# A gated linear attention layer and its GELU MLP on one core: a scheduled two-stage kernel rewritten as a hand-ordered two-phase pipeline with transposes by DMA

## The chip, the cores and the metric

The kernel runs on one core of a Trainium2 chip. The core has five engines with instruction streams of their own: PE (TensorE, matrix products; PEld is its loading of weights), ACT (ScalarE), DVE (VectorE), POOL (GpSimd) and SP (SyncE, which here only issues DMAs). Sixteen DMA engines carry out the transfers that SP and POOL issue. The metric is device time in microseconds (us), as the median of several executions; lower is better.

## The reference

Inputs are q, k, v and alpha of shape (batch 4, heads 8, sequence 768, head size 48) in float32, and two weights, w_in (384 x 2048) and w_out (2048 x 384). The heads of the result lie side by side and make rows of 384 for the MLP:

```python
for t in range(S):                       # S = 768, per batch and head
    state = alpha[t][:, None] * state + outer(k[t], v[t])      # 48 x 48
    y[t]  = q[t] @ state
x = y.transpose(0, 2, 1, 3).reshape(3072, 384)
h = x @ w_in                             # 3072 x 2048
g = 0.5 * h * (1 + tanh(c * (h + 0.044715 * h**3)))
out = g @ w_out                          # 3072 x 384
```

## The kernel before, in words

The sequence is cut into chunks of 128 steps. A unit is one chunk of one batch element with all 8 heads: 6 chunks by 4 batch elements are 24 units, taken in the order "all four batch elements of chunk 0, then of chunk 1, ...". With b the running product of alpha inside a chunk, a unit computes q' = q b and k' = k / b, the masked scores (k' q'^T, causal), y = scores v + q' state, and the new state = (state + k'^T v) b_end.

The kernel has two stages one after the other, and then a drain.

- **Decays, all units at once** (lines 99 to 122). For each pair of units alpha is loaded by POOL (L105), its logarithm is taken on ACT (L108, with a constant MU folded in against overflow), and PE sums it along the chunk with a triangular matrix `ut` (L114, tile `cumla`) and per head with a column of ones (L118). DVE keeps the sums in `cum_all` (L120), ACT keeps exp of the end sums in `bend_all` (L121). `w_in` and `w_out` are loaded by SP in float32 (L93, L130) and cast to bf16 by DVE (L127, L159).
- **Units in a three-step software pipeline** (lines 146 to 178). Stage a loads q, k, v by POOL (L190). Stage b makes exp of the sums on ACT (L200, L202), the products q' and k' on DVE (L205, L206), casts v on ACT (L208), and transposes q' and k' per head on PE (L213, L214), with a copy out of PSUM by ACT (L215) and DVE (L216). Stage c makes the scores on PE (L234), masks them on DVE (L237, tile `atm`), makes y and the state's increment on PE (L241, L243, L245), updates the state on DVE (L249, L250), copies y to `x_sb` on ACT (L255), transposes it on PE (L259) and copies it on DVE into `xT_all` (L260).
- **The MLP** runs in groups of four units (512 rows) as a list of pieces: 16 first-layer pieces (three matmuls L275 into `hT`, GELU on ACT L279 into `gT`) and 4 second-layer pieces (16 matmuls L286 into `acc`, a DVE copy L291, an SP store L293). After each unit up to 7 pieces are popped from the list; what is left is drained at the end.

Instructions are written in this order, and a scheduler sets the final order on each engine. Buffers come from pools; the PSUM buffers `tT_ps`, `ybank` and `acc` are single.

## Time and profile before

| what | value |
|---|---|
| time, median of 3 runs | 298.85 us (297.84 to 299.3) |
| span of the profiled execution, first to last instruction | 295.8 us |
| median time less that span | 3.05 us |
| busy: PE, ACT, DVE, POOL | 224.5, 200.8, 141.3, 87.4 us |
| DMA: bytes moved, mean rate over the span | 30.22 MB, 102 GB/s |

The page gives no time of its own for the profiled execution, only its span; the 3.05 us are what the timed runs hold beside such a span. Busy time is what an engine spent in instructions; matmuls overlap in the pipeline, so the mean duration of one (379 ns for L275) is longer than the distance from one to the next. "Idle before" is the engine's idle time just ahead of a group of instructions, with what ended it. The chain of waits follows the last instruction back to what released it. "L275" is line 275 of the kernel.

### The profile page before, as it was taken

What the parts mean: (1) busy time and instruction counts of PE and PEld (TensorE: products, weight loads), DVE (VectorE), ACT (ScalarE), POOL (GpSimd) and SP (SyncE); (2) the same over time, 40 slices, a digit from 0 to 9 for tenths busy, and PEclk for the clock granted to TensorE, in tenths of its full rate; (3) what the DMA queues carried; (4) which work ended last, traced back from release to release, by engine and by line L of the source; (5) the groups of instructions that cost most, each with busy time, mean ns of one, the idle gap of its engine ahead of it and who ended that gap; (6) DMA issues with size and microseconds to landing.
All of it is one profiled execution on the core that took longest, in us unless ns stands there. A gap on an engine that the chain in (4) does not pass through costs nothing.

```text
span 295.8 us, 5241 instructions
## 1 busy us (share of the span) xinstructions
PE 224.5 (76%) x2112; PEld 132.8 (45%) x2112; DVE 141.3 (48%) x274; ACT 200.8 (68%) x301; POOL 87.4 (30%) x114
## 2 busy tenths in 40 slices
PE   0043333332778989899998999999999999999983
PEld 0022212221656535556556555565456644554441
DVE  7183433222599855567548144656243633540011
ACT  0257787978677999996999999945761276304800
POOL 9643321005988758153333213220000000000000
PEclk9999999999999999999999999999999999999999
DMA  7999951002999979373232512241001100011011
GB/s 278 283 187 274 291 126 53 0 1 67 193 187 187 189 144 198 89 181 99 80 82 59 182 53 55 53 109 53 2 1 55 53 2 0 3 53 55 0 53 54
DMA packets 12168, 30.22 MB, mean 102 GB/s; under 512 B 2032, under 2 KB 7152, under 8 KB 11760
## 3 DMA queue, kind: packets, MB, share of 16 engines
q0 software_dynamic: 6144, 18.88, 30.4%
q1 hardware_dynamic: 6000, 11.01, 11.0%
q8 instruction: 16, 0.26, 0.4%
q14 instruction: 8, 0.07, 0.1%
HBM read 25.17 MB, written 4.72 MB: 101 GB/s over the span
## 4 chain that ended last, share of the span: by engine, by line
PE 47%; ACT 34%; DMA 7%; DVE 6%; issue 3%; POOL 1%; SPq 0%; DVEq 0%; POOLq 0%; ACTq 0%
PE acc L286 16%; PE hT L275 15%; ACT gT L279 6%; ACT L279 5%; ACT L108 4%; DMA w_in_f<-in_moe_w_in_dram 4%; ACT qT_ring L215 3%; PE kT_ps L214 3%; PE qT_ps L213 3%; ACT la L108 3%; PE at_ps L234 2%; ACT L200 2%; ACT L202 2%; ACT L121 2%; DVE w_in_sb L127 2%
## 5 line engine op out<-in xcount | busy, mean ns | idle before, releaser
L275 PE MATMUL hT<-xT_all,w_in_sb 128*128 128x512 bf16 x288 | 74.5, 379 | 4.0 <-ACT gT L279 3.8
L286 PE MATMUL acc<-w_out_sb,gT 128*128 128x384 bf16 x384 | 70.8, 326 | 3.0 <-DVE ot L291 2.8
L279 ACT ACTIVATE gT<-hT 128x512 bf16<-128x512 f32 x96 | 55.5, 598 | 16.3 <-PE hT L275 14.2
L286 PEld LDWEIGHTS <-gT 128*128 128x128 bf16 x384 | 36.4, 97 | 28.0 <-issue 4.0
L114 PE MATMUL cumla<-la,ut 128*128 128x384 bf16 x24 | 11.6, 485 | 48.3 <-ACT la L108 39.1
L291 DVE COPY ot<-acc 128x384 f32<-128x384 f32 x24 | 13.3, 555 | 53.6 <-PE acc L286 53.6
L237 DVE TENSOR_TENSOR atm<-at_ps,ut 128x512 bf16<-128x512 f32 x48 | 31.1, 683 | 15.9 <-PE at_ps L234 15.7
L275 PEld LDWEIGHTS <-w_in_sb 128*128 128x128 bf16 x288 | 24.8, 97 | 26.3 <-issue 5.5
L118 PEld LDWEIGHTS <-la 128*48 128x48 bf16 x192 | 9.5, 129 | 55.5 <-issue 55.5
L190 POOL DMA_DIRECT2D q<-in_q_dram x24 | 21.2, 884 | 44.1 <-PE cumla L118 24.1
L120 DVE CAST cum_all<-cumla 128x384 f16<-128x384 f32 x24 | 13.3, 556 | 32.5 <-PE cumla L118 32.5
L190 POOL DMA_DIRECT2D v<-in_v_dram x24 | 21.2, 885 | 25.3 <-ACT v8b L208 21.8
L105 POOL DMA_DIRECT2D a<-in_alpha_dram x24 | 21.5, 900 | 21.3 <-ACT la L108 18.9
L215 ACT COPY qT_ring<-qT_ps 64x1024 bf16<-64x1024 bf16 x24 | 24.1, 1005 | 4.9 <-PE qT_ps L213 4.6
L190 POOL DMA_DIRECT2D k<-in_k_dram x24 | 21.2, 885 | 18.3 <-DVE kp_ring L206 17.4
L208 ACT CAST v8b<-v 128x384 bf16<-128x384 f32 x24 | 12.3, 512 | 18.7 <-PE yps L243 17.9
L216 DVE COPY kT_ring<-kT_ps 64x1024 bf16<-64x1024 bf16 x24 | 16.3, 680 | 17.5 <-PE kT_ps L214 17.1
L108 ACT ACT_TABLE_LOAD x11 | 14.1, 1283 | 13.4 <-DMA a<-in_alpha_dram 13.2
L213 PE MATMUL qT_ps<-ident,qp_ring 128*64 128x128 bf16 x192 | 18.3, 230 | 5.9 <-DVE qp_ring L205 5.3
L205 DVE TENSOR_TENSOR qp_ring<-q,b 128x384 bf16<-128x384 f32 x24 | 13.2, 551 | 14.6 <-PE at_ps L234 5.7
L213 PEld LDWEIGHTS <-qp_ring 128*64 128x64 bf16 x192 | 12.7, 114 | 16.5 <-issue 14.9
L255 ACT CAST x_sb<-yps 128x384 bf16<-128x384 f32 x24 | 11.4, 476 | 12.7 <-PE yps L243 10.6
(49 smaller groups left out, 319.2 us busy)
## 6 DMA issues: line engine op xcount, KB each, us to landing
a<-in_alpha_dram POOLq DMA_DIRECT2D x24, 192.0 KB, 7.2
q<-in_q_dram POOLq DMA_DIRECT2D x24, 192.0 KB, 5.3
k<-in_k_dram POOLq DMA_DIRECT2D x24, 192.0 KB, 5.7
v<-in_v_dram POOLq DMA_DIRECT2D x24, 192.0 KB, 5.2
out_dram<-ot SPq DMA_DIRECT2D x24, 192.0 KB, 1.9
w_in_f<-in_moe_w_in_dram SPq DMA_DIRECT2D x3, 1024.0 KB, 7.4
w_out_f<-in_moe_w_out_dram SPq DMA_DIRECT2D x4, 768.0 KB, 12.4
```

Source lines behind the costliest of these rows:

```text
L105: nc.gpsimd.dma_start(a8[:, i], alpha[b].rearrange("h s d -> s h d")[tsl])
L108: nc.scalar.activation(la8, a8, AF.Ln, scale=float(math.exp(-MU)))
L120: nc.vector.tensor_copy(cum_all[:, tt, :], cumla)
L190: nc.gpsimd.dma_start(t_sb, t_dram[b].rearrange("h s d -> s h d")[tsl])
L213: nc.tensor.transpose(qT_ps[:, h, :], qp[:, h, :], ident)
L215: nc.scalar.copy(qT[0:64], qT_ps)
L216: nc.vector.tensor_copy(kT[0:64], kT_ps)
L237: nc.vector.tensor_tensor(atm, at_ps, ut[:, None, :].to_broadcast([C, 4, C]), op=ALU.mult)
L275: nc.tensor.matmul(hT, w_in_sb[:, j, nt * C:(nt + 1) * C], xsl, start=(j == 0), stop=(j == NKT - 1),)
L279: nc.scalar.activation(gT[:, nt, :], hT, AF.Gelu_apprx_tanh)
L286: nc.tensor.matmul(acc, gT[:, nt, mt * C:(mt + 1) * C], w_out_sb[:, nt, :], start=(nt == 0), stop=(nt == NFT - 1),)
L291: nc.vector.tensor_copy(ot, acc)
```

## The change

The kernel is written anew with the same mathematics and the same tiling into units and groups.

- **Order.** No scheduler: each engine runs its instructions as the program emits them. There is no separate decay stage. Per group of four units the program has two phases. Phase 1 merges the second layer of the group before (16 pieces of 4 matmuls, `layer2`) with this group's state update and y (`kv`, `y`) and the next group's decays (`e_ln`, `e_cum`, `e_exp`) and transposes of q' and k' (`t_qk`). Phase 2 merges this group's first layer (`layer1`, 16 pieces) with the next group's scores (`attn`). `_merge` spreads the side work over the main pieces at fixed places.
- **Transposes.** q', k' (128 x 512 with the heads padded to 64, bf16) and x (128 x 384) are transposed by DMAs from SBUF to SBUF that SP issues: 2 per unit for q' and k', 1 per unit for x. The PE transposes and the copies out of PSUM are gone.
- **Heads in pairs.** After the transpose two heads lie on partitions 0 to 63 and 64 to 127. Scores of the two heads are matmuls on 64 rows each; the state's increment, the end sums and q' state are done for two heads in one matmul.
- **Casting DMAs.** v, `w_in` and `w_out` are loaded by POOL straight into bf16. The first two groups' alpha, q and k are loaded by SP, all later loads by POOL, two groups ahead.
- **Decays.** Pairs of units are handled in one ACT instruction; Ln and Exp come from one function set that the program loads itself; the sums are used straight from PSUM; the logarithms are float16 and MU is gone. The first chunk has no q' state product and the last no state update.

Three places of the order, as the two programs have it on the engines concerned.

ACT in the decay stage before (`la` is the logarithm, `bend_all` the end factors):

```order
L108 ACT_TABLE_LOAD
L108 ACTIVATE la_206<-a_203 128x768
L121 ACT_TABLE_LOAD
L121 ACTIVATE bend_all<-cumla,bias_end 48x8 x3
L108 ACT_TABLE_LOAD
L108 ACTIVATE la_235<-a_232 128x768
L121 ACT_TABLE_LOAD
```

and now, from the logarithms of the next group to the first GELUs of this one:

```order
L120 ACTIVATE la_99<-a_286 128x16x48
L219 CAST x<-yps 128x384
L120 ACTIVATE la_100<-a_298 128x16x48
L219 CAST x<-yps 128x384
L141 ACTIVATE b_694<-cum 128x768
L142 ACTIVATE binv_695<-cum 128x768
L143 ACTIVATE bend<-cum 128x8
L219 CAST x<-yps 128x384 x2
L141 ACTIVATE b_787<-cum 128x768
L142 ACTIVATE binv_788<-cum 128x768
L143 ACTIVATE bend<-cum 128x8
L239 ACT_TABLE_LOAD
```

Before, each pair switches the function table twice; now a group of four units does so twice, and x copies stand between and behind the exponentials.

SP, the whole program before:

```order
L93 DMA w_in_f_135<-in_moe_w_in_dram 128x2048 x3
L130 DMA w_out_f_494<-in_moe_w_out_dram 128x4x384 x4
L293 DMA out_dram<-ot 128x384 x24
```

and now at the start, with the semaphores that each row waits for (DMAHW0 to 7 are eight completion lanes, used in turn):

```order
L93 DMA q_175<-in_q_dram 128x8x48 [waits DMAHW4_49]
L93 DMA q_175<-in_q_dram 128x8x48 [waits DMAHW5_49]
L93 DMA k_178<-in_k_dram 128x8x48 [waits DMAHW6_49]
L93 DMA k_178<-in_k_dram 128x8x48 [waits DMAHW7_49]
L158 DMA_TRANSPOSE qkT<-qp_103 128x4x128 [waits DMAHW0_49,DVE_49,Pool_49]
L159 DMA_TRANSPOSE qkT<-kp_107 128x4x128 [waits DMAHW1_49,DVE_49,Pool_49]
L158 DMA_TRANSPOSE qkT<-qp_103 128x4x128 [waits DMAHW2_49]
L159 DMA_TRANSPOSE qkT<-kp_107 128x4x128 [waits DMAHW3_49]
```

SP issued weights and stores only; now 24 loads stand ahead of the first transpose, and a DMA cannot be issued before the one eight places ahead of it has landed.

SP in a later group, now (phase 1 of group 2):

```order
L221 DMA_TRANSPOSE xT<-x 128x3x128 [waits DMAHW4_49,Activation_49]
L258 DMA out_dram<-ot 128x384 [waits DMAHW5_49,DVE_49]
L221 DMA_TRANSPOSE xT<-x 128x3x128 [waits DMAHW6_49,Activation_49]
L221 DMA_TRANSPOSE xT<-x 128x3x128 [waits DMAHW7_49,Activation_49]
L258 DMA out_dram<-ot 128x384 [waits DMAHW0_49,DVE_49]
L221 DMA_TRANSPOSE xT<-x 128x3x128 [waits DMAHW1_49,Activation_49]
L158 DMA_TRANSPOSE qkT<-qp_105 128x4x128 [waits DMAHW2_49,PE_49]
L159 DMA_TRANSPOSE qkT<-kp_109 128x4x128 [waits DMAHW3_49]
```

Here 12 transposes and 4 stores per group share one queue, in which the four x transposes of a group come before the eight of q' and k' of the next.

The diff, cut to the new functions (the removed lines are those of the kernel before):

```diff
--- before.py
+++ after.py
...
+LN_EXP_SET = 6
+DMA_QK = True
+DMA_X = True
...
+    with ExitStack() as ctx, tc.manual_schedule():
+        _Kernel(ctx, tc, q, k, v, alpha, moe_w_in, moe_w_out, out).run()
...
+def _merge(main, side, first=0.0, last=1.0):
+
+    n, m = len(main), len(side)
+    lo, hi = first * n, last * n
+    at = [lo + (hi - lo) * (i + 0.5) / m for i in range(m)] if m else []
+    j = 0
+    for i in range(n):
+        while j < m and at[j] <= i:
+            side[j]()
+            j += 1
+        main[i]()
+    while j < m:
+        side[j]()
+        j += 1
...
+        self.state = [[const.tile([C, H // 2, 2 * D], BF16, name=f"st{b}_{i}") for i in range(2)]
+                      for b in range(B)]
+        self.NR = 4
+        self.la_ring = [const.tile([C, 2, H, 64], F16, name=f"la{i}") for i in range(self.NR)]
+        self.qp_ring = [const.tile([C, 2, H, 64], BF16, name=f"qp{i}") for i in range(self.NR)]
+        self.kp_ring = [const.tile([C, 2, H, 64], BF16, name=f"kp{i}") for i in range(self.NR)]
...
+    def load(self, names, pair, eng):
+        for n in names:
+            dt = F32 if n != "v" else BF16
+            t = self.ld.tile([self.C, 2, self.H, self.D], dt, tag=n + "8", bufs=6 if n == "v" else 4, name=n + "8")
+            for i, (c, b) in enumerate(pair):
+                sl = slice(c * self.C, (c + 1) * self.C)
+                e = eng if n != "v" else self.nc.gpsimd
+                e.dma_start(t[:, i], self.src[n][b].rearrange("h s d -> s h d")[sl])
+                self.u.setdefault((c, b), {})[n] = t[:, i]
+            self.u[pair[0]][n + "pair"] = t
...
+        self.nc.gpsimd.dma_start(
+            self.w_in[:, :, sl], self.w_in_dram.rearrange("(j c) n -> c j n", c=self.C)[:, :, sl])
...
+    def e_ln(self, pair):
+        u0 = self.u[pair[0]]
+        r = u0["ring"] = self.npair % self.NR
+        self.npair += 1
+        self.nc.scalar.activation(self.la_ring[r][:, :, :, 0:self.D], u0["apair"], AF.Ln)
...
+        cum = u0["cum"] = self.ps.tile([self.C, 2, 512], F32, tag="ca", name="cum")
+        for i in range(2):
+            nc.tensor.matmul(cum[:, i, 0:H * D], self.ut_h, la[:, i, :, 0:D], start=True, stop=True)
+            for p in range(H // 2):
+                nc.tensor.matmul(cum[:, i, H * D + p:H * D + p + 1],
+                                 la[:, i, 2 * p:2 * p + 2, :].rearrange("t h d -> t (h d)"),
+                                 self.ones, start=True, stop=True, skip_group_check=True)
...
+        nc.scalar.activation(b8, cum[:, :, 0:H * D], AF.Exp)
+        nc.scalar.activation(binv8, cum[:, :, 0:H * D], AF.Exp, scale=-1.0)
+        nc.scalar.activation(bend, cum[:, :, H * D:H * D + H // 2], AF.Exp)
+        qp, kp = self.qp_ring[r], self.kp_ring[r]
+        nc.vector.tensor_tensor(qp[:, :, :, 0:D], u0["qpair"],
+                                b8.rearrange("t i (h d) -> t i h d", h=H), op=ALU.mult)
+        nc.vector.tensor_tensor(kp[:, :, :, 0:D], u0["kpair"],
+                                binv8.rearrange("t i (h d) -> t i h d", h=H), op=ALU.mult)
...
+        t = self.grp.tile([C, 2, H // 2, C], BF16, tag="qkT", bufs=8, name="qkT")
+        if DMA_QK:
+            nc.sync.dma_start_transpose(t[:, 0], u["qp"].rearrange("t h d -> t (h d)"))
+            nc.sync.dma_start_transpose(t[:, 1], u["kp"].rearrange("t h d -> t (h d)"))
...
+        at = self.ps.tile([C, 2, H // 2, C], F32, tag="ca", name="at")
+        for p in range(H // 2):
+            for o in range(2):
+                sl = slice(64 * o, 64 * o + 64)
+                nc.tensor.matmul(at[:, o, p, :], kT[sl, p, :], qT[sl, p, :], start=True, stop=True)
+        atm = u["atm"] = self.grp.tile([C, 2, H // 2, C], BF16, tag="atm", bufs=6, name="atm")
+        for o in range(2):
+            nc.vector.tensor_tensor(atm[:, o], at[:, o],
+                                    self.ut[:, None, :].to_broadcast([C, H // 2, C]), op=ALU.mult)
...
+        kv = self.ps.tile([C, H // 2, 2 * D], F32, tag="yk", bufs=2, name="kv")
+        for p in range(H // 2):
+            nc.tensor.matmul(kv[:, p, :], u["kp"][:, 2 * p:2 * p + 2, :].rearrange("t h d -> t (h d)"),
+                             u["v"][:, 2 * p:2 * p + 2, :].rearrange("t h d -> t (h d)"),
                              start=True, stop=True)
+        old, new = self.state[b][c % 2], self.state[b][(c + 1) % 2]
+        for o in range(2):
+            ps, fs = slice(64 * o, 64 * o + 64), slice(D * o, D * o + D)
+            acc = kv[ps, :, fs]
+            if c > 0:
+                s = self.wk.tile([C, H // 2, D], F32, tag=f"stmp{o}", name="stmp")
+                nc.vector.tensor_tensor(s[ps], acc, old[ps, :, fs], op=ALU.add)
+                acc = s[ps]
+            nc.vector.tensor_tensor(new[ps, :, fs], acc,
+                                    u["bend"][ps, :, None].to_broadcast([64, H // 2, D]), op=ALU.mult)
...
+        yps = self.ps.tile([C, H, D], F32, tag="yk", bufs=2, name="yps")
+        if c > 0:
+            st = self.state[b][c % 2]
+            for p in range(H // 2):
+                nc.tensor.matmul(yps[:, 2 * p:2 * p + 2, :], u["qT"][:, p, :], st[:, p, :],
+                                 start=p == 0, stop=False, skip_group_check=True)
+        for h in range(H):
+            nc.tensor.matmul(yps[:, h, :], u["atm"][:, h % 2, h // 2, :], u["v"][:, h, :],
+                             start=c == 0, stop=True, skip_group_check=True)
+        x = self.wk.tile([C, H * D], BF16, tag="x", name="x")
+        nc.scalar.copy(x, yps.rearrange("t h d -> t (h d)"))
+        if DMA_X:
+            nc.sync.dma_start_transpose(xT[:, :, i, :], x)
...
+            h = self.ps.tile([C, N * C], F32, tag="ff", bufs=4, name="hT")
+            for j in range(self.NKT):
+                nc.tensor.matmul(h, self.w_in[:, j, nt * C:(nt + 1) * C],
+                                 xT[:, j].rearrange("p g t -> p (g t)"),
+                                 start=j == 0, stop=j == self.NKT - 1)
+            nc.scalar.activation(gT[:, nt, :], h, AF.Gelu_apprx_tanh)
...
+                acc[mt] = self.ps.tile([C, self.d_model], F32, tag="ff", bufs=4, name="acc")
+            for nt in range(part * 4, part * 4 + 4):
+                nc.tensor.matmul(acc[mt], gT[:, nt, mt * C:(mt + 1) * C], self.w_out[:, nt, :],
+                                 start=nt == 0, stop=nt == self.NFT - 1)
+            if part == self.NFT // 4 - 1:
+                ot = self.wk.tile([C, self.d_model], F32, tag="ot", name="ot")
+                nc.vector.tensor_copy(ot, acc[mt])
+                c, b = group[mt]
+                r = b * self.S + c * C
+                nc.sync.dma_start(self.out[r:r + C, :], ot)
...
+        pairs = [[g[0:2], g[2:4]] for g in G]
+        self.act_set(LN_EXP_SET)
+        for p in pairs[0]:
+            self.load("aqk", p, nc.sync)
+        for i in range(self.NR):
+            self.pads(i)
+        for p in pairs[0]:
+            self.load("v", p, nc.gpsimd)
+        for b in range(self.B):
+            for i in range(2):
+                nc.vector.memset(self.state[b][i], 0.0)
+        for p in pairs[1]:
+            self.load("a", p, nc.sync)
+        for i in range(4):
+            self.load_w_in(i, 4)
+        for p in pairs[1]:
+            self.load("qk", p, nc.sync)
+            self.load("v", p, nc.gpsimd)
+
+        def decays(pp):
+            return ([lambda p=p: self.e_ln(p) for p in pp],
+                    [lambda p=p: self.e_cum(p) for p in pp],
+                    [lambda p=p: self.e_exp(p) for p in pp])
+
+        ln, cum, exp = decays(pairs[0])
+        for f in (ln[0], ln[1], cum[0], exp[0]):
+            f()
+        for cb in pairs[0][0]:
+            self.t_qk(cb)
+        cum[1]()
+        exp[1]()
+        for cb in pairs[0][1]:
+            self.t_qk(cb)
+        for cb in G[0]:
+            self.attn(cb)
+
+        gT_prev = None
+        for g in range(len(G)):
+            more = g + 1 < len(G)
+            xT = self.grp.tile([self.C, self.NKT, len(G[g]), self.C], BF16, tag="xT", name="xT")
+            gT = self.grp.tile([self.C, self.NFT, len(G[g]) * self.C], BF16, tag="gT", name="gT")
+
+            side = []
+            if more:
+                if g + 2 < len(G):
+                    side.append(lambda: [self.load("aqkv", p, nc.gpsimd) for p in pairs[g + 2]])
+                ln, cum, exp = decays(pairs[g + 1])
+                side += [lambda: self.act_set(LN_EXP_SET), ln[0]]
+                side += [lambda: self.yk(G[g][0], xT, 0), ln[1]]
+                side += [lambda: self.yk(G[g][1], xT, 1), cum[0], exp[0]]
+                side += [lambda: self.yk(G[g][2], xT, 2)]
+                side += [lambda: self.yk(G[g][3], xT, 3), cum[1], exp[1]]
+                side += [lambda cb=cb: self.t_qk(cb) for cb in G[g + 1]] if DMA_QK else []
+            else:
+                side += [lambda i=i: self.yk(G[g][i], xT, i) for i in range(4)]
+            if g == 0:
+                side.append(lambda: [self.load_w_out(i, 4) for i in range(4)])
+            main = self.layer2(G[g - 1], gT_prev) if g else []
+            _merge(main, side, 0.0, 0.8)
+
+            side = []
+            if more:
+                for cb in G[g + 1]:
+                    if not DMA_QK:
+                        side.append(lambda cb=cb: self.t_qk(cb))
+                    side.append(lambda cb=cb: self.attn(cb))
+            _merge(self.layer1(xT, gT), side, 0.1, 1.0)
+            gT_prev = gT
+        for f in self.layer2(G[-1], gT_prev):
+            f()
+
+    def yk(self, cb, xT, i):
+        self.kv(cb)
+        self.y(cb, xT, i)
```

370 lines of the change are left out of this document (108 added, 262 removed).

## The prediction, made before the result was known

> **What bounds the kernel now.** I read busy time by stage first, then the chain of waits, then the durations that the sum needs. In the stages below the columns are the stretch, its length and the busy time of each engine with its instructions; then the granted TensorE clock (1.00 is full), the busy share of the DMA engines and the GB/s that they moved.
>
> ```profile
> span 295.8 us, 5241 instructions
> 0.00:70.00 70.00, 21.04 (x216) 12.03 (x216) 28.68 (x58) 44.41 (x58) 24.03 (x43) 1.00 0.59 158
> 70.00:100.00 30.00, 20.36 (x296) 16.20 (x297) 22.70 (x44) 23.73 (x43) 26.97 (x31) 1.00 0.97 180
> 100.00:293.00 193.00, 183.12 (x1601) 104.56 (x1599) 89.87 (x172) 132.61 (x204) 36.38 (x42) 1.00 0.27 70
> ```
>
> There are three regimes. For 70 us PE is idle two thirds of the time (21.0 us busy). From 70 to 100 the DMA engines are full (0.97). From 100 on PE is busy 183 of 193 us. The chain shows what holds the first stage:
>
> ```profile
> 60.71 1.28 ACT L108
> 62.01 0.85 ACT la L108
> 64.70 1.28 ACT L108
> 66.00 0.84 ACT la L108
> 66.86 1.28 ACT L121
> 69.92 0.88 POOL q L190
> 72.55 4.38 DMA q<-in_q_dram
> ```
>
> Per pair ACT pays 1.28 us for a table, 0.84 for a logarithm and 1.28 for the table back; the next pair waits for that round. q's first load is issued only when the stage ends (69.92), and lands 4.4 us after its issue. So the first 70 us are a latency chain that carries no MLP work, and what follows is PE throughput.
>
> **What the change does to PE.** Dense stretches of PE give prices (start, duration with the pipeline's fill, what):
>
> ```profile
> 199.88 2.76 PE L286 MATMUL acc<-w_out_sb,gT 128*128 128x384 bf16 x16
> 202.48 0.19 PE L241 MATMUL yps<-v8b,atm 128*128 128x48 bf16 x1
> 202.86 0.18 PE L243 MATMUL yps<-state_b,qT_ring 128*128 128x48 bf16 x1
> 202.89 1.02 PE L275 MATMUL hT<-xT_all,w_in_sb 128*128 128x512 bf16 x4
> 204.80 0.62 PE L234 MATMUL at_ps<-qT_ring,kT_ring 128*128 128x128 bf16 x8
> 205.35 0.23 PE L245 MATMUL kv<-v8b,kp_ring 128*48 128x48 bf16 x2
> ...
> 272.07 1.49 PE L275 MATMUL hT<-xT_all,w_in_sb 128*128 128x512 bf16 x6
> 273.40 0.33 PE L286 MATMUL acc<-w_out_sb,gT 128*128 128x384 bf16 x1
> 273.56 1.49 PE L275 MATMUL hT<-xT_all,w_in_sb 128*128 128x512 bf16 x6
> ```
>
> From start to start: a second-layer matmul is 2.60/16 = 0.163 us; a first-layer one (1.49 - 0.16)/6 = 0.222; 16 matmuls of y 0.41, so 0.026 each; the 8 scores of a unit 0.55. The MLP alone is thus 288 x 0.222 + 384 x 0.163 = 126.5 us, and PE's other work now fills most of the rest of its 224.5. The change removes 384 + 72 PE transposes, 96 end-sum matmuls, and more than half of the increments and state products (192 each, now 80 each of 96 columns). [...]
>
> - phase 2: 48 x 0.222 + 4 x 0.55 = 12.9 us (10.7 in the last group, which has no scores to make);
> - phase 1: 64 x 0.163 = 10.4, plus per unit 8 x 0.026 + 4 x 0.05 for y, 4 x 0.05 for the increment and about 0.4 for the sums (a 384-column matmul and four tiny ones), so 1.0 x 4, plus 1.0 for y waiting on the x copies, which stand behind two exponentials on ACT: 15.4.
>
> ACT and DVE stay below that. The rows that price them:
>
> ```profile
> L279 ACT ACTIVATE gT<-hT 128x512 bf16<-128x512 f32 x96 | 55.5, 598 | 16.3 <-PE hT L275 14.2
> L108 ACT ACTIVATE la<-a 128x768 bf16<-128x768 f32 x12 | 10.0, 841 | 0.1
> L237 DVE TENSOR_TENSOR atm<-at_ps,ut 128x512 bf16<-128x512 f32 x48 | 31.1, 683 | 15.9 <-PE at_ps L234 15.7
> L205 DVE TENSOR_TENSOR qp_ring<-q,b 128x384 bf16<-128x384 f32 x24 | 13.2, 551 | 14.6 <-PE at_ps L234 5.7 <-DMA q<-in_q_dram 5.2 <-PE qT_ps L213 1.1
> L255 ACT CAST x_sb<-yps 128x384 bf16<-128x384 f32 x24 | 11.4, 476 | 12.7 <-PE yps L243 10.6 <-PE hT L275 2.0
> L121 ACT ACT_TABLE_LOAD x11 | 14.1, 1283 | 0.2
> ```
>
> ACT in phase 2: 16 x 0.598 + 1.28 = 10.9 of 12.9 us; in phase 1: 1.28, six 768-wide functions at 0.84, four x copies at 0.476, two small ones: 8.8 of 15.4. DVE in phase 2: 8 x 0.683 = 5.5. The copies out of PSUM that go (L215, L216, L260, L120, the casts) were hidden behind PE after 100 us, so removing them gains nothing by itself.
>
> From the first first-layer matmul to the end: 5 x 12.9 + 10.7 + 5 x 15.4 + a last second layer of 10.4 + 3.7 for the last copy and store,
>
> ```profile
> 292.07 0.56 DVE L291 COPY ot<-acc 128x384 f32<-128x384 f32 x1 [2.85 <-PE acc L286]
> ```
>
> (292.07 to 295.8 now), together 166.3 us.
>
> **What the change adds: 72 transposes on SP's queue.** The trace has no DMA transpose. Call T the time that one of q' or k' holds the queue (x, three quarters as wide, 0.75 T). Rows near it:
>
> ```profile
> q0 software_dynamic: 6144, 18.88, 30.4%
> ...
> q<-in_q_dram POOLq DMA_DIRECT2D x24, 192.0 KB, 5.3
> ```
>
> The 96 loads are 98,304 runs of 192 bytes in 30.4% of 16 x 295.8 us: 14.6 ns per run. The lower bound of T takes the 128 KB of a transpose in runs of 256 bytes (one row of a 128-column block): 512 x 14.6/16 = 0.47 us. The upper bound is the 5.3 us to landing of a 192 KB load, as if transposes ran one by one. [...]
>
> [...]
>
> **Where T counts.** In a group, the products for the first pair of the next group are ready about 5 us before phase 2: behind its sums stand 40 second-layer matmuls, two units, the second pair's sums and the 1.0 us of waits, 9.5 us, less two exponentials and the small one (1.9) and two products (2 x 1.1). The last scores stand after 45 of the 48 first-layer matmuls and three other scores, 11.6 us into phase 2. Taking off one landing and two stores in between (row below: a store is issued in 0.33 us and lands in 1.9), 14 us are left for eight transposes. So up to T = 1.75 they are hidden behind PE, and beyond it PE waits 8T - 14 in each of five groups; behind the waiting scores PE's remaining first-layer matmuls are queued, and behind these ACT's GELUs.
>
> ```profile
> L293 SPq DMA_DIRECT2D out_dram<-ot x24: 332/332/361, 122.7 to 292.7; - x24
> DMA to landing us min/median/max: 1.8/1.9/5.0
> ```
>
> The x transposes run ahead of those in the queue and have 32 matmuls and a pair of sums, 6 us, before the first layer needs them; 0.75 T + 1.9 fits.
>
> **The start.** The first transposes come behind SP's 24 loads, and POOL's eight v loads and w_in compete. Rates with the DMA engines full, in two stretches: 75 to 100 (192-byte runs alone), and 0 to 20 in slices of 0.5 us (mostly w_in from 3 to 8):
>
> ```profile
> DMA packets 1520, 4.70 MB, mean 188 GB/s; under 512 B 378, under 2 KB 378, under 8 KB 1518
> ...
> GB/s 0 0 0 131 98 213 459 410 410 442 377 410 426 410 427 394 397 337 249 335 364 263 320 267 255 231 180 188 190 195 183 168 202 174 203 182 203 165 177 183
> ```
>
> 32 loads of 196,608 bytes at 188 GB/s are 33.5 us, w_in's 3.15 MB at 410 are 7.7, and 2 pass before data flows: 43 us. I take casting at no cost; by bytes it could go up to twice the time of v and w_in, 16 us more. If SP's 24 loads went first it would be 27 us; if POOL's sixteen loads for group 2 also went ahead (16.7 us), 60. Then 8T for the transposes, 1.9 to land, 1.4 for the masks of a unit, 6 for four units of y with the next pair's exponentials between, and T + 1.9 for the last x: 9T + 11.2.
>
> **Sum.** Span = 43 + 9T + 11.2 + 166.3 + 5 x max(0, 8T - 14); with T = 1.9, 43 + 17.1 + 11.2 + 166.3 + 6 = 243.6 us. The profiled span is 295.8 and the median 298.85, so 3.05 lie around it in the median run, and I add these: 247 us. Compared with now, the 70 us chain and the 30 us behind it become some 71 us before the MLP starts, and the 193 us of PE become about 172.
>
> **Rivals.**
>
> - *The transposes set the pace* (slower). If each holds SP's queue for the 5.3 us of a landed load, a group needs 8 x 5.3 + 4 x 4.0 + 4 x 0.33 = 60 us of SP against 28.3 of PE: 43 + 9 x 5.3 + 11.2 + 5 x 60 + 10.7 + 10.4 + 3.7 + 3 = 430 us. Past T = 1.75 the sum is 153.6 + 49T, so it decides from T = 2.95, where it reaches 298.85. For it: every transpose moves small pieces, and POOL's loads share the engines. Against it: eight in flight. [...]
> - *The DMA engines become the bound.* If the 1.9 us are time of all 16 engines: 18.87 MB of loads at 188 GB/s are 100 us, weights 15 and stores 11.5 at 410, transposes 66 x 1.9 = 125; with 2 us at the start and 25 at the end, when nothing is left to load, 280 us. For it: the full share from 70 to 100. Against it: 0.27 afterwards, and loads two groups ahead.
> - *The start is slow but the rest as forecast*: 60 in place of 43, 264 us.
> - That the change does nothing is excluded by the order: the decay stage is gone.
>
> **How the numbers follow.** Forecast mechanism (PE paced, T up to 2.3) 0.55, with its own range 226 to 267; slow start 0.08; DMA bound 0.16; transposes setting the pace 0.21, of which about 0.05 lie below 315. The range 226 to 315 leaves out some 0.16 above and 0.03 below. What a measurement can tell from no change is about 0.5%, 1.5 us. Faster: 0.55 + 0.08 + 0.16 less 0.01 = 0.78; slower 0.21 less 0.01 = 0.20; same 0.02, since the two outer cases meet 298.85 only in passing.
>
> **What would show it.** Right: eight transposes issued at the start from about 43 us on, first-layer matmuls from about 70, PE over 85% busy from then on, no wait of scores (`at`) for DMAs above 2 us, 11 table loads. Wrong: scores or the first layer waiting for `qkT` or `xT` in every group (T above 1.75), DMA share near 1 through the middle (DMA bound), or the first transposes later than 60 us. The step I trust least is T; one row of the new trace, the issue-to-issue distance of transposes that wait for nothing else, settles it.

## The result, and the profile after

| | time, median | span of the profiled execution | ratio to before, 95% interval |
|---|---|---|---|
| before | 298.72 us (297.84 to 299.3) | 295.8 us | |
| after | 282.76 us (282.64 to 287.19) | 280.8 us | 0.946 (0.9433 to 0.9488) |

The change makes the kernel 16 us faster. The forecast was 52 us faster; two thirds of that did not come. Now and then an execution is 1.5% or more longer than the quickest of its kernel; the ratios leave such ones out, and the profiled executions of e2, e8 and e10 further on are of this kind (2.0, 1.5 and 2.4% longer).

The page of the changed kernel, its busy times and three rows of its 40 slices (7.0 us each; in the row PEclk 9 is 90% or more of the full clock):

```profile
span 280.8 us, 3547 instructions
...
PE 166.2 (59%) x1325; PEld 90.4 (32%) x1336; DVE 93.4 (33%) x177; ACT 110.6 (39%) x179; POOL 74.1 (26%) x102
...
PE   1010000000252739977299782699799989999995
...
PEclk9999999999999987999779999599999999999999
DMA  9999999999428993189980799972352235232002
```

PE's work fell from 224.5 to 166.2 us, but PE now idles 41% of the span. The slices show where: the first ten, in which the DMA engines are full, and then three holes, at 98, 133 and 168 us (slices 14, 19 and 24, counted from 0: a 3 and two 2s). Each hole has a 9 in the DMA row; in slices 16 and 21, between the holes, that row falls to 1 and 0 while PE is at 9. The last loads are issued at 169 us, in the third hole, and from 183 us on PE is full but for a 7 and an 8, until the end.

SP's queue of the changed kernel, the rows that carry the start and the steps (start, time that the row holds the queue, what, how many):

```profile
18.14 15.22 SPq L93 DMA_DIRECT2D a<-in_alpha_dram  x4
...
57.72 9.07 SPq L93 DMA_DIRECT2D k<-in_k_dram  x2
66.92 1.29 SPq L158 DMA_TRANSPOSE qkT<-qp  x1
68.32 1.19 SPq L159 DMA_TRANSPOSE qkT<-kp  x1
...
76.11 1.26 SPq L159 DMA_TRANSPOSE qkT<-kp  x1
...
95.33 5.41 SPq L159 DMA_TRANSPOSE qkT<-kp  x1
```

The first transpose goes out at 66.92 us (forecast: 43). When little else moves (103 GB/s in all from 70 to 78 us), eight transposes start 1.31 us apart ((76.11 - 66.92)/7); at 95.33 one holds the queue for 5.41 us. What moves beside them is POOL's, in the rows of its queue:

```profile
18.50 0.89 POOL L93 DMA_DIRECT2D a<-in_alpha_dram  x1 [1.86 <-DMA w_in<-in_moe_w_in_dram]
...
48.49 1.49 POOL L106 DMA_DIRECT2D w_out<-in_moe_w_out_dram  x2 [0.73 <-DMA q<-in_q_dram]
50.62 1.78 POOL L93 DMA_DIRECT2D a<-in_alpha_dram  x2 [0.64 <-DMA k<-in_k_dram]
84.72 1.76 POOL L93 DMA_DIRECT2D q<-in_q_dram  x2 [32.32 <-DVE qp L145]
...
116.79 1.79 POOL L93 DMA_DIRECT2D a<-in_alpha_dram  x2 [19.74 <-ACT la L120]
...
154.13 1.78 POOL L93 DMA_DIRECT2D a<-in_alpha_dram  x2 [19.86 <-ACT la L120]
```

From 18.50 to 46 us POOL issues the 16 loads of group 2, then `w_out`, then two alpha loads of group 3: only free buffers and the landing of earlier transfers hold these back, nothing that the first transposes need. Later loads go out in bursts, from 84.72, 116.79 and 154.13, as soon as the logarithm or q' has read the old buffer. PE's rows after each burst (in brackets the idle time just before, and what ended it):

```profile
92.77 0.58 PE L236 MATMUL hT<-xT,w_in 128*128 128x512 bf16 x1 [5.36 <-DMA xT<-x]
...
103.76 0.61 PE L177 MATMUL at<-qkT 64*128 64x128 bf16 x8 [4.36 <-DMA qkT<-kp]
104.30 5.30 PE L236 MATMUL hT<-xT,w_in 128*128 128x512 bf16 x12
...
139.49 0.61 PE L177 MATMUL at<-qkT 64*128 64x128 bf16 x8 [5.58 <-DMA qkT<-kp]
...
178.07 0.61 PE L177 MATMUL at<-qkT 64*128 64x128 bf16 x8 [7.83 <-DMA qkT<-kp]
```

So in each of the phases 2 of groups 0 to 2 the scores of one unit wait for its transposed k', 4.4 to 7.8 us long, with the first layer queued behind them. Stretches of the same trace (columns as in the prediction):

```profile
92.77:104.30 11.53, 6.95 (x37) 2.80 (x38) 1.29 (x2) 4.18 (x7) 4.28 (x5) 0.93 1.40 168
104.30:107.00 2.70, 2.70 (x9) 1.04 (x8) 1.29 (x2) 0.60 (x1) 0.00 (x0) 0.50 1.64 161
107.00:116.00 9.00, 8.95 (x64) 4.14 (x63) 2.71 (x5) 6.41 (x10) 0.00 (x0) 0.86 0.02 4
...
134.00:139.40 5.40, 0.00 (x0) 0.00 (x0) 0.00 (x0) 0.55 (x1) 0.27 (x1) 0.76 1.20 176
...
204.60:216.70 12.10, 11.99 (x80) 5.27 (x80) 4.97 (x8) 8.96 (x15) 0.00 (x0) 1.00 0.43 99
216.70:231.92 15.22, 14.06 (x149) 9.25 (x148) 11.72 (x25) 9.72 (x15) 0.00 (x0) 1.00 0.29 70
```

PE and the DMA engines largely take turns. At 134 PE does nothing at all while 176 GB/s flow; at 107 PE is full while 4 GB/s flow. The last two rows are a phase 2 and a phase 1 after the last load: 12.1 and 15.2 us, against 12.9 and 15.4 in the forecast.

### The profile page after: what moved, and what is told of

It reads as the page before. It is cut to its first block, busy times and chain, and to the rows that moved or that the text cites. A ratio compares the mean times of both kernels' runs of the same rounds, so it can differ in the third digit from the quotient of the medians.

```text
span 280.8 us, 3547 instructions
## 1 busy us (share of the span) xinstructions
PE 166.2 (59%) x1325; PEld 90.4 (32%) x1336; DVE 93.4 (33%) x177; ACT 110.6 (39%) x179; POOL 74.1 (26%) x102
## 3 DMA queue, kind: packets, MB, share of 16 engines
q1 hardware_dynamic: 64512, 18.10, 38.4%
## 5 line engine op out<-in xcount | busy, mean ns | idle before, releaser
L236 PE MATMUL hT<-xT,w_in 128*128 128x512 bf16 x277 | 72.9, 409 | 9.2 <-DMA xT<-x 8.0
L180 DVE TENSOR_TENSOR atm<-at,ut 128x512 bf16<-128x512 f32 x48 | 30.9, 686 | 112.7 <-PE at L177 112.7
L251 PE MATMUL acc<-w_out,gT 128*128 128x384 bf16 x384 | 67.9, 325 | 0.0
L177 PE MATMUL at<-qkT 64*128 64x128 bf16 x192 | 11.0, 243 | 78.3 <-DMA qkT<-kp 78.3
L236 PEld LDWEIGHTS <-w_in 128*128 128x128 bf16 x288 | 28.0, 103 | 44.7 <-issue 17.9
L219 ACT CAST x<-yps 128x384 bf16<-128x384 f32 x24 | 11.5, 479 | 62.5 <-PE yps L216 60.5
L255 DVE COPY ot<-acc 128x384 f32<-128x384 f32 x24 | 13.4, 557 | 34.4 <-PE acc L251 34.1
L93 POOL DMA_DIRECT2D v<-in_v_dram x24 | 21.5, 910 | 6.3 <-DMA v<-in_v_dram 5.7
L120 ACT ACTIVATE la<-a 128x768 f16<-128x768 f32 x12 | 10.1, 844 | 29.4 <-DMA a<-in_alpha_dram 29.4
L145 DVE TENSOR_TENSOR qp<-q,b 128x768 bf16<-128x768 f32 x12 | 11.5, 959 | 23.0 <-ACT b L141 16.8
L200 DVE TENSOR_TENSOR stmp<-kv,st 64x192 f32<-64x192 f32 x32 | 11.4, 355 | 6.9 <-PE kv L191 6.3
L147 DVE TENSOR_TENSOR kp<-k,binv 128x768 bf16<-128x768 f32 x12 | 11.4, 951 | 5.5 <-DMA k<-in_k_dram 5.5
L202 DVE TENSOR_TENSOR st<-stmp,bend 64x192 bf16<-64x192 f32 x32 | 11.3, 352 | 1.1
```

Of the source, the lines that this page charges most:

```text
L93: e.dma_start(t[:, i], self.src[n][b].rearrange("h s d -> s h d")[sl])
L145: nc.vector.tensor_tensor(qp[:, :, :, 0:D], u0["qpair"], b8.rearrange("t i (h d) -> t i h d", h=H), op=ALU.mult)
L147: nc.vector.tensor_tensor(kp[:, :, :, 0:D], u0["kpair"], binv8.rearrange("t i (h d) -> t i h d", h=H), op=ALU.mult)
L177: nc.tensor.matmul(at[:, o, p, :], kT[sl, p, :], qT[sl, p, :], start=True, stop=True)
L180: nc.vector.tensor_tensor(atm[:, o], at[:, o], self.ut[:, None, :].to_broadcast([C, H // 2, C]), op=ALU.mult)
L200: nc.vector.tensor_tensor(s[ps], acc, old[ps, :, fs], op=ALU.add)
```

## The experiments

The miss has two places, the start and three phases, and the same suspect in both: loads of a later group that run ahead of the transposes (start) or beside them (phases). The rivals are that the transposes are slow in themselves or badly placed in SP's queue, and that PE loses its time to the lower clock after each wait. All kernels below are the changed kernel with the edit shown; each quoted expectation sets two explanations against each other. Ratios are to the kernel before on the same chip.

| run | time, us | ratio (95%) | first transpose | first first-layer matmul | from there to the end | span |
|---|---|---|---|---|---|---|
| after | 282.76 | 0.946 (0.943 to 0.949) | 66.9 | 92.8 | 188.0 | 280.8 |
| e3_no_later_loads | 235.38 | 0.786 (0.784 to 0.788) | 49.5 | 72.3 | 162.0 | 234.3 |
| e1_later_qk | 277.29 | 0.925 (0.919 to 0.930) | 34.4 | 92.5 | 183.7 | 276.2 |
| e2_gated_prefetch | 269.76 | 0.899 (0.897 to 0.902) | 41.3 | 68.0 | 204.4 | 272.4 |
| e7_gated_bursts | 268.21 | not given | 48.8 | 71.8 | 194.0 | 265.8 |
| e8_filler | 284.23 | 0.948 (0.942 to 0.953) | 67.3 | 93.9 | 190.9 | 284.8 |
| e4_qk_by_pe | 257.92 | 0.862 (0.860 to 0.863) | x only, 68.8 | 80.8 | 175.3 | 256.1 |
| e5_x_by_pe | 300.10 | 1.003 (0.999 to 1.006) | 66.8 | 90.4 | 209.0 | 299.4 |
| e6_both_by_pe | 266.26 | 0.889 (0.884 to 0.894) | none | 66.5 | 199.1 | 265.6 |
| e9_mended_start | 223.32 | 0.747 (0.745 to 0.749) | x only, 37.1 | 52.4 | 169.2 | 221.6 |
| e10_mended_start_qk_dma | 259.67 | 0.860 (0.855 to 0.864) | 18.0 | 61.7 | 198.2 | 259.9 |
| e11_mended_start_no_gate | 237.51 | 0.795 (0.793 to 0.797) | x only, 38.2 | 54.3 | 181.5 | 235.8 |

The last four columns are of the profiled execution.

### e3_no_later_loads: the suspect taken away

The loads of groups 2 to 5 are left out; those groups compute on the data of groups 0 and 1, so the output is not the reference's, and all other work is done.

```diff
+        self.kept = {cb: dict(self.u[cb]) for cb in G[0] + G[1]}
...
-                    side.append(lambda: [self.load("aqkv", p, nc.gpsimd) for p in pairs[g + 2]])
+                    side.append(lambda: [self.reuse(p) for p in pairs[g + 2]])
```

> Leaves out the loads of groups 2 to 5 (64 of the 96); those groups compute on the data of groups 0 and 1. All compute, all transposes and all stores stay. Theory A: the start is 40 to 48 us, no scores wait for transposes after it, the granted clock is 1.00 from the first layer on, and the time is 222 to 236 us. Rival B (transposes slow by themselves): the start shortens, the waits of scores in groups 1 to 3 stay (5 to 8 us each), 245 to 262 us. Rival C (the clock is low for a reason other than the waits): no waits, but first-layer matmuls at 0.44 us as now in places, above 236.

Measured: 235.38 us, 47 us less than after and in the range of theory A; the start, 49.5 us, is just outside its 40 to 48, since `w_out` is still loaded ahead of it. The landing of all 48 q'/k' transposes, first in the changed kernel and then here, and here PE's longest wait for them:

```profile
DMA to landing us min/median/max: 2.4/4.1/14.1
```

```profile
DMA to landing us min/median/max: 2.4/2.5/4.4
```

```profile
PE at L177 <- DMA qkT<-kp: 41.9, 4, 36.0
...
72.34 5.28 PE L236 MATMUL hT<-xT,w_in 128*128 128x512 bf16 x12 [2.26 <-DMA xT<-x]
```

All four waits of the scores belong to the start; the three in the phases are gone, and the granted clock is 1.000 on the mean. (The last row is taken up in the section on the hardware.) The transposes are the same 72 in the same queue; without loads beside them none lands later than 4.4 us. That the transposes are slow in themselves is out. Loads do have to be made, however, so this says where the time goes and not that it can be had.

### e1_later_qk: the place in SP's queue

Group 1's eight q and k loads stand behind the first eight transposes instead of ahead of them.

```diff
         for p in pairs[1]:
-            self.load("qk", p, nc.sync)
             self.load("v", p, nc.gpsimd)
...
         for cb in pairs[0][1]:
             self.t_qk(cb)
+        for p in pairs[1]:
+            self.load("qk", p, nc.sync)
```

> Only SP's order changes: the eight loads of q and k of group 1 stand behind the first eight transposes in place of ahead of them. Theory A (what stands ahead in bytes sets the start, and loads running beside the transposes slow them; a transpose alone costs about 1.25 us): the first transpose goes out at about 45 us in place of 66.9, the first first-layer matmul at about 71 in place of 92.8, and the time is about 262 us (255 to 270), with the stalls of scores in the first three groups unchanged. Rival B (the transposes are slow by themselves, through their eight lanes and their own cost on SP's queue): the start moves, but the eight transposes still take as long, and little comes of it: 272 to 283.

Measured: 277.29 us, 5 us less. SP's rows, and PE's first first-layer row:

```profile
34.41 5.16 SPq L158 DMA_TRANSPOSE qkT<-qp  x1
39.68 2.93 SPq L159 DMA_TRANSPOSE qkT<-kp  x1
42.67 5.81 SPq L158 DMA_TRANSPOSE qkT<-qp  x1
...
79.13 9.29 SPq L221 DMA_TRANSPOSE xT<-x  x4
...
92.53 4.47 PE L236 MATMUL hT<-xT,w_in 128*128 128x512 bf16 x12 [11.34 <-DMA xT<-x]
```

The transposes went out 32 us earlier, and the first four then held the queue for 2.9 to 5.8 us each, beside POOL's loads; the x transposes came behind the moved loads, and the first first-layer matmul stands at 92.53, where it was. So the estimate that saw a gain of 12 us and more was wrong. The time lies in the range of rival B, whose reason (transposes slow in themselves) e3 excludes: the place in SP's queue only decides which transposes wait, those of q' and k' or those of x, while the same loads stand ahead of the first layer.

### e2_gated_prefetch: fewer bytes ahead of the start

A one-column copy on POOL, which reads the last transposed k' of group 0, stands ahead of group 2's loads and so of `w_out` as well.

```diff
+                    if g == 0:
+                        side.append(lambda: self.gate())
                     side.append(lambda: [self.load("aqkv", p, nc.gpsimd) for p in pairs[g + 2]])
...
+    def gate(self):
+        t = self.grp.tile([self.C, 1], BF16, tag="gate", name="gate")
+        self.nc.gpsimd.tensor_copy(t, self.u[self.groups[0][3]]["kT"][:, 0, 0:1])
```

> One small POOL copy that reads the last transposed tile of group 0 stands ahead of POOL's loads for group 2, so these and w_out wait until the first transposes have landed. Theory A: SP's 24 loads, eight v loads and w_in are then all that runs before, 43 us by the prediction's own rates (40 to 48), and the first transpose goes out there in place of 66.9; the loads held back run later beside the transposes of group 1, so part of the gain is given back: 258 to 270 us. Rival B: POOL's loads do not matter to SP's queue, first transpose still after 60, 278 to 285.

Measured: 269.76 us, in the range of theory A. Now exactly the 32 loads and `w_in` of the forecast go ahead, and the first transpose stands at 41.33 (forecast 43):

```profile
41.33 1.54 SPq L158 DMA_TRANSPOSE qkT<-qp  x1
```

The start is mended by 25 us, but only 13 arrive at the end. The bytes that were held back collide one phase later, where PE's wait for x was 1.8 us after the change:

```profile
118.19 5.06 PE L236 MATMUL hT<-xT,w_in 128*128 128x512 bf16 x12 [12.52 <-DMA xT<-x]
```

### e7_gated_bursts: every burst behind the transposes

The same copy for each group, reading the last transposed k' of the next group, and `w_out` ahead of group 2. The copy and the loads stand between the two phases of the program.

```diff
+        for i in range(4):
+            self.load_w_out(i, 4)
...
-                if g + 2 < len(G):
-                    side.append(lambda: [self.load("aqkv", p, nc.gpsimd) for p in pairs[g + 2]])
...
             _merge(main, side, 0.0, 0.8)
...
+            if g + 2 < len(G):
+                self.gate(G[g + 1][3])
+                for p in pairs[g + 2]:
+                    self.load("aqkv", p, nc.gpsimd)
```

> All transposes stay with the DMAs and all bytes stay. w_out is loaded right behind group 1's v, and POOL's sixteen loads for group g+2 wait (by a small POOL copy that reads the last transposed tile) until the transposes of group g+1 have landed, so that loads and transposes of q' and k' take turns. Theory A: the first transposes go out at about 50 us as without the later loads, the scores' waits of 4 to 8 us in three groups go, and the time is 238 to 254 us. Rival B (transposes slow by themselves): waits stay, above 258. Rival D (16.7 us of loads do not fit between two sets of transposes): functions and products wait for late loads instead, 255 to 270.

Measured: 268.21 us (264.75 to 271.09). No scores wait for a transpose after the start. A new wait has their place, on ACT, for the alpha of the group that comes next, and through ACT's copies of x behind it on PE:

```profile
ACT la L120 <- DMA a<-in_alpha_dram: 56.1, 8, 15.3
...
PE kv L191 <- ACT x L219: 25.2, 8, 6.1
```

In the changed kernel the two rows have 29.4 us in three waits, all at the start, and 2.5 us. This is rival D, in its range and by its mechanism: held behind all eight transposes the loads come too late. In this program a burst has to have ended before the next transposes (the changed kernel's scores waited 4.4 to 7.8 us for those beside one), and to have begun early enough for the next logarithm (the 56.1 us here): what counts is where in the group it stands.

### e8_filler: the clock

Behind the three long waits the first-layer matmuls of the changed kernel run slower, at worst at half rate: 12 in 5.30 us at 104.30, 9 in 3.88 at 140.03 and 9 in 3.37 at 178.61, with a granted clock of 0.50 to 0.60; elsewhere 12 take 2.76 (at 144.17) and 9 take 2.12 (at 97.28). Here PE runs 24, 20, 24 and 32 products of 512 columns into an unused buffer just ahead of the instructions that wait.

```diff
+            if g == 0:
+                self.filler(24)
...
-                    side.append(lambda cb=cb: self.attn(cb))
+                    n = {(0, 1): 20, (1, 0): 24, (2, 0): 32}.get((g, cb[1]), 0)
+                    if n:
+                        side.append(lambda cb=cb, n=n: (self.filler(n), self.attn(cb)))
+                    else:
+                        side.append(lambda cb=cb: self.attn(cb))
```

> 100 matmuls of 512 columns whose result nobody reads stand on PE where it now waits for DMAs: 24 ahead of the first first-layer matmul, 20 ahead of group 1's second scores, 24 and 32 ahead of the first scores of groups 2 and 3. They do not shorten any wait. Theory C (the granted clock is low after a wait, 0.50 to 0.60 in these stretches, and matmuls cost twice): the first-layer matmuls behind the waits run at 0.22 us in place of 0.30 to 0.44, and the time falls to 273 to 279 us. Rival (those matmuls are slow because DMA traffic takes memory ports): they stay slow, 282 to 286.

Measured: 284.23 us, ratio 0.9475 (0.9422 to 0.9528) against 0.946 of the change: no difference. Yet the rate is back where the hole was filled (the last row is the stretch, with PE's busy time, clock, DMA share and GB/s):

```profile
99.45 4.48 PE L346 MATMUL fill<-w_in 128*128 128x512 bf16 x20
104.09 0.40 PE L177 MATMUL at<-qkT 64*128 64x128 bf16 x8 [0.16 <-DMA qkT<-kp]
104.42 2.76 PE L236 MATMUL hT<-xT,w_in 128*128 128x512 bf16 x12
...
100.00:107.00 7.00, 6.84 (x39) 1.00 1.50 152
```

Twelve matmuls take 2.76 us again, in the same place, beside the same traffic: from 104 to 107 us the granted clock is 1.00 at 165 GB/s, where the changed kernel has 0.50 at 161. There the clock still reads 0.58 from 107 to 110, when 3 GB/s flow. So in these runs the half rate goes with the clock behind an idle PE and not with the loads beside it. It costs nothing here that the time shows. The first layer of group 1 begins 2.5 us sooner (128.69 against 131.17), but the scores of group 2 again wait for their transposes until 140.66 (139.49 in the changed kernel): what PE wins it seems to lose at the next landing. The test is not complete, for in that hole the fill ran out 4.0 us early and the clock fell again (0.57 from 141 to 145). The expectation of a gain was wrong, and so was the reason that the rival gave for none, though its range was right.

### e4_qk_by_pe, e5_x_by_pe, e6_both_by_pe: which transposes belong where

The kernel has two switches. Off, the transposes are PE's, through PSUM, with a DVE copy.

```diff
-DMA_QK = True
+DMA_QK = False
```

in e4; `DMA_X = False` in e5; both in e6.

> q' and k' are transposed on PE in pairs of heads (8 per unit) with one DVE copy of 128x1024 out of PSUM per unit; x stays with the DMAs. Theory A: PE pays 0.5 to 0.6 us per unit, 12 to 14 in all, but scores no longer wait for DMAs (78 us of waits now, 54 of them the start); x transposes still stand behind SP's 24 loads, so the first layer starts at about 72 in place of 92.8; 248 to 262 us. Rival: the copies out of PSUM and the shared PSUM buffers make waits of the same size, and nothing is won beyond the start: 265 to 280.

> x is transposed on PE (3 per unit) and copied out of PSUM by DVE; q' and k' stay with the DMAs. Theory A (loads beside the transposes): the first transposes still go out at about 67 us; the four x transposes and their landing leave the start (5 to 7 us), the 2.6 us that first layers later wait for xT go, PE pays about 6 us more, and the waits of scores stay: 274 to 281 us. Rival B (each transpose costs SP's queue by itself): 24 of 72 fewer should free a third of the waits, 8 us or more beyond the start: below 272.

> All transposes on PE, none by DMA; loads as in the changed kernel. Theory A: nothing waits for a transpose any more, and what is left of the slow start is the loads themselves: the first layer starts at about 70 us, because group 1's q and k land only at about 67 and DVE makes their products ahead of group 0's last state updates; afterwards PE is busy throughout with some 18 us more of its own work: 245 to 256 us. Rival: the copies out of PSUM (24 of 128x1024, 24 of 128x384 on DVE) and the shared PSUM buffers stall PE, and it is no better than with x by DMA: 258 or more.

Measured: 257.92, 300.10 and 266.26 us. q' and k' by PE saves 25 us although PE does 9.5 us more (175.7 busy). x by PE loses 17 in one case and 8 in the other. e4 is in the range of its theory A; theory A was too low in e5 and e6, and e6 lies in its rival's range (258 or more). PE's waits in e4, e5 and e6:

```profile
PE hT L236 <- DMA xT<-x: 16.5, 3, 11.8
```

```profile
PE at L177 <- DMA qkT<-kp: 81.3, 8, 54.3
PE xT_ps L225 <- ACT x L219: 17.0, 24, 1.4
```

```profile
PE xT_ps L225 <- ACT x L219: 20.4, 24, 4.2
PE kv L191 <- DVE st L202: 15.0, 1, 15.0
```

A transpose of x on PE stands in PE's order right behind the product that it needs, and waits for ACT's copy of it: 24 times 0.7 us in e5, 17.0 in all. That is not the whole account of e5: PE is also busy 11.3 us longer, and 8.0 us of waits for x by DMA are gone. In e6 the same wait is 20.4 us, while 16.5 of e4's are gone. The same transpose by DMA lets PE go on. One of q' and k' on PE is free to stand in the middle of the first layer, because its products are long done (no such transpose waits there in e4); by DMA it falls into the burst. So the three places seem to differ more by what PE would wait for than by the price of a transpose. The 15.0 us of e6 are one wait at the start, for a state update of group 0 that DVE runs behind group 1's products; e4 has the like, 17.5 us. The next kernels change that order.

### e9, e10, e11: the loads put where they disturb nothing

e9 has q' and k' by PE, x by DMA, and moves only loads and one group's order: ahead of the first products only group 0's loads and `w_in`; group 0's products ahead of group 1's decays; and each later group's loads behind a copy that reads that phase's last transposed x, so that a burst begins when the x transposes have landed and runs beside the first layer.

```diff
-        for p in pairs[1]:
-            self.load("a", p, nc.sync)
         for i in range(4):
             self.load_w_in(i, 4)
+        self.gate(self.u[G[0][3]]["k"][:, 0, 0:1])
+        for n in ("a", "qkv"):
+            for p in pairs[1]:
+                self.load(n, p, nc.gpsimd)
+        for i in range(4):
+            self.load_w_out(i, 4)
...
+                if g == 0:
+                    side += [lambda i=i: self.yk(G[0][i], xT, i) for i in range(4)]
+                    side += [lambda: self.fetch(g + 2, pairs, xT)]
+                    side += [ln[0], ln[1], cum[0], exp[0], cum[1], exp[1]]
...
+                    side += [lambda: self.yk(G[g][3], xT, 3)]
+                    side += [lambda: self.fetch(g + 2, pairs, xT)]
...
+    def fetch(self, g, pairs, xT):
+        if g < len(self.groups):
+            if GATE:
+                self.gate(xT[:, 0, 3, 0:1])
+            for p in pairs[g]:
+                self.load("aqkv", p, self.nc.gpsimd)
```

e10 is e9 with `DMA_QK = True`, all transposes where the change has them. e11 is e9 with `GATE = False`: the start stays, the later bursts are free again.

> q' and k' transposed by TensorE as in e4; x by DMA. Changed beside that: only group 0's loads and the first-layer weights go ahead of the first products (group 1's loads and the second-layer weights wait on POOL behind a copy that reads group 0's last k tile), group 0's products stand ahead of group 1's decays, and the loads of each later group wait behind a copy that reads that phase's last transposed x tile. Theory (the miss of the prediction is the set of loads that run ahead of and beside the transposes): 16 loads of 196,608 B at 188 GB/s and 3.15 MB at 410 are 24 us, with the chain of decays, scores and products the first first-layer matmul starts between 38 and 50; from there on as in e4, whose stretch from the first first-layer matmul to the end is 175 us; together 215 to 232 us with 3 around the span, below every kernel so far that does all of the work. Rival (the loads' rate and not their place sets the time, held-back loads are missing later as in e7): 245 to 265 us, with waits of the decays' ACT for alpha loads.

> As e9_mended_start, but q' and k' by DMA transposes as in the changed kernel, so that all transposes stand as the change has them and only the loads have been moved. Theory: transposes that stand beside a burst of loads are late, and here the loads of the group after next start just when the eight q'/k' transposes are issued, so scores wait again for qkT by 4 to 8 us in groups 0 to 2: 10 to 30 us above e9, 230 to 260. Rival (order of the loads is all that counts, the transposes themselves are free): within 3 us of e9 or below it by up to 8, since PE has 10 us less to do.

> As e9_mended_start without the copies that hold the later groups' loads behind the x transposes (the start stays mended: the one copy on group 0's last k tile stays). Theory: the later loads run as soon as their buffers are free, so the x transposes of groups 0 to 2 share the DMA engines with them, and the first layer waits up to 12 us for xT in group 0 and 1 to 5 us after: 3 to 15 us above e9. Rival: the same time as e9, within 2 us, since e4 has no wait for xT over 5 us after its first group.

Measured: 223.32, 259.67 and 237.51 us; all three in the range of the first theory. e9 is the quickest kernel of this study, a quarter below the kernel before and 59 us below the change. Stretches of e9 from its first first-layer matmul on, a first layer and a second one in turn:

```profile
52.40:67.00 14.60, 14.19 (x95) 7.06 (x98) 6.37 (x10) 8.58 (x15) 14.25 (x17) 1.00 1.21 187
67.00:82.00 15.00, 13.97 (x158) 9.07 (x156) 11.04 (x24) 8.79 (x15) 0.34 (x1) 1.00 0.61 90
82.00:97.00 15.00, 14.76 (x112) 7.79 (x113) 8.97 (x13) 10.59 (x19) 14.70 (x17) 1.00 1.05 179
```

In the first and the third PE is busy 97 and 98% with the DMA engines full (187 and 179 GB/s): both run at once, where the changed kernel had them take turns. In e10 PE's waits for the transposes of q' and k' are back:

```profile
PE at L178 <- DMA qkT<-kp: 50.1, 12, 11.3
```

Of these, 26.1 us are the start's four and 24 the phases'; the rest of e10 behind the first first-layer matmul is 29 us longer than e9's, and its start 9.3, together 38 in the profiled execution where the ratios give 34. e11 shows the same for x (waits of the first layer, in e9 2.7 us altogether), and the longest of its waits:

```profile
PE hT L237 <- DMA xT<-x: 12.6, 4, 6.6
...
91.48 0.58 PE L237 MATMUL hT<-xT,w_in 128*128 128x512 bf16 x1 [6.58 <-DMA xT<-x]
```

By the ratios, the gates of e9 alone are worth 14 us (0.7947 less 0.747 of 298.57) and q' and k' on PE 34 (0.8595 less 0.747). Loads and the one group's order by themselves are worth 26 us with the change's own transposes (0.946 less 0.8595, e10) and 34 with q' and k' on PE (0.8615 less 0.747, e9 against e4). The table shows where: at the first first-layer matmul e9 is 28 us ahead of e4 and e10 31 ahead of the change, but from there to the end e9 gains only 6 and e10 loses up to 10: its scores wait 24 us there, the change's 17.8, since the bursts again stand beside the transposes of q' and k'.

## Why the prediction was right or wrong

**Right: the direction, and PE's prices.** Phase 2 was forecast at 12.9 us and measured at 12.1, phase 1 at 15.4 and 15.2. The 0.8 us are the scores: a unit's eight, on 64 rows each, were put at 0.55 us and take 0.33 (from 143.84 to 144.17 in the changed kernel). From the first first-layer matmul to the end the forecast without stalls was 166.3; e3, where neither scores nor first layer wait for a transpose in that stretch, took 162.0. The 70 us chain of table loads is gone; 11 table loads are left, as forecast. Of the signs named for a wrong forecast, the first transposes behind 60 us came. Scores waiting for `qkT` came too, but in three groups of five, and not with the T above 1.75 that was given as their cause. PE was busy 83% from the first layer on (156.8 of 188.0 us), just short of the 85 named for a right one.

**Too high, and lucky: T.** No run shows the T of 1.9 us that the sum uses; it was my estimate. What the runs show in its place is 1.31 us, the distance of transposes that wait for nothing else, between the bounds of 0.47 and 5.3. With 1.31 the sum is 235 us, 12 further from the measured 282.76, so this error hid part of the two below. The packets come close to the lower bound's runs of 256 bytes (the queue of SP in the changed kernel and in e4):

```profile
q1 hardware_dynamic: 64512, 18.10, 38.4%
...
q1 hardware_dynamic: 38400, 11.80, 26.4%
```

That is 26,112 packets fewer in e4, for 48 transposes of 131,072 bytes: 544 each, of 241 bytes. With T = 1.31 the formula hides all eight, and e3 agrees with its terms: 9T + 11.2 = 23.0 against 72.3 - 49.5 = 22.8. 131,072 bytes each 1.31 us are 100 GB/s from this queue, and 103 flowed in all from 70 to 78 us.

**Wrong, first step: "43 us" until the first transposes.** The rates were right and the set of transfers was not. I counted SP's 24 loads, eight v loads and `w_in`. Ahead of 66.9 us there also went 16 loads of group 2, two alphas of group 3 and `w_out`: 50 x 196,608 bytes at 188 GB/s are 52.3 us, 6.3 MB at 410 are 15.3, and with the 2 us before data flows 69.6 in all. The text named 16 of these loads and gave their case a chance of 0.08, though the order of the program put them right behind the v loads, where only free buffers and the landing of earlier transfers held them. With the set that I had counted (e2) the step is right, 41.3. This is 21.5 us of the 37 that the span came out above the forecast: 23.9 at the first transpose, less 2.4 that the following chain was shorter.

**Wrong, second step: T as a constant, in "5 x max(0, 8T - 14)".** Beside a burst one transpose held the queue for 5.41 us, one landed only 14.1 us after its issue, and the stall came to 26.0 us over the three groups that have loads beside them (188.0 against 162.0) where the term had 6.0 over five. Of the 26.0, the scores' three waits are 17.8 and those of the first layer for x 2.6; matmuls at the lower clock behind the waits make up about the rest (12 in 5.30 us, 9 in 3.88 and 9 in 3.37, against 2.76 and 2.12). The estimated T gave a stall of the right kind for a wrong reason, and spread it over groups 3 and 4, which have none. What failed is that I priced transposes and loads each alone, on DMA engines that they share; whether it is the engines themselves or something behind them that holds a transpose up, no run separates. The two misses, 21.5 and 15.7 (188.0 against 172.3), are the 37.2 us of the span.

**The rivals.** "The DMA engines become the bound" said 280 us, beside 280.8 of span, yet it was not its mechanism: it had the engines full throughout, with 1.9 us of all 16 for each transpose. Measured, the queue that holds the transposes loses 40.2 us of packet time in e4 (38.4% of 280.8 less 26.4% of 256.1), 0.84 us for each of 48, and the share falls to 0.02 between bursts. e9 moves the same loads, with the x transposes, in 221.6 us. "The transposes set the pace" is refuted by e3. "Slow start" was half of the truth, its 60 us still 7 short.

**Small: 3.05 us around the span.** The profiled executions that have a time of their own show 1.8 (282.64 less 280.8); I had taken the difference of a median and another execution's span.

## What to carry to other kernels

The prefetch that only its buffers held back went out here from 18.50 us on, as soon as they were free, and the first transposes, which the critical path needed next, came at 66.92 us in place of 43: in a forecast, count what every queue will have issued by then, not what the path needs. Before replacing a compute engine's transposes by DMAs, ask what else moves at that moment. Those of q' and k' landed at most 4.4 us after their issue without the later loads (e3), and up to 14.1 us with them (the changed kernel), while PE was 97 and 98% busy beside loads in two first layers of e9 (187 and 179 GB/s). So try to give a transfer on the path a stretch without bulk loads, and bulk loads the stretch in which the compute engines need nothing new. Moving the loads, with one group's order, was worth more here (26 to 34 us, most of it at the start) than the whole rewrite had brought (16).

## What the runs showed of the hardware

- In the changed kernel the granted TensorE clock was 0.50 from 104.3 to 107 us, behind an idle of 4.36 us, and matmuls of the first layer took twice their time for some 5 us (12 in 5.30 against 2.76); with the hole filled (e8) it was 1.00 from 104 to 107. Behind the three waits it read 0.58 from 107 to 110, 0.54 from 139.4 to 144 and 0.60 from 178 to 182, and 1.00 again from 110 to 113.5, 144 to 150 and 182 to 188: full again some 4 to 6 us after PE went on.
- The clock's record does not show every slow stretch. In e3 the twelve first first-layer matmuls take 5.28 us, twice the 2.76 of twelve at 80.25, while the clock is 1.000 on the mean. I had not thought of slow matmuls, since the kernel before shows 1.00 nearly throughout (0.998 on the mean); its durations had them, for L114's 384 columns take 479 ns until 68.5 us, and L286's 384 columns 326 later. What slows these two stretches is not shown.
- With the DMA engines full SP's queue was held 15.22 us by four loads at 18.14 (171 GB/s) and 5.41 us by one transpose at 95.33 (182 GB/s); the eight transposes from 66.92 on, with little beside them, held it 1.19 to 1.29 us each. In e1, beside POOL's loads, one held it 5.81 us.
- In e9 matmuls of the first layer run at the full rate beside loads: six take 1.47 us at 65.33 ((1.47 - 0.16)/6 = 0.22 each), with 187 GB/s from 52.4 to 67 us. No loss by the traffic shows there.
